# Keys and queries of three blocks loaded in 1 KB runs, with a re-made instruction plan

## The chip, the cores and the metric

The kernel runs on one core of a Trainium2 chip. The metric is the device time of one execution in microseconds (us), as the median of several executions. The profiled span is 1.8 to 1.9 us shorter than that time. The engines are PE (matmul), DVE (vector), ACT (scalar), POOL (GpSimd, which here writes the descriptors of the casting loads) and SP (which here issues stores and transposing DMAs). A single core gives no second die to compare with, so an execution counts as slow only if it is over 1.5% above the fastest; one execution of the kernel before was (317.86 us), and it is left out of every ratio.

## The reference

Sliding-window attention with a distance bias, then a feed-forward layer with a squared ReLU on its result:

```python
q, k, v: (8, 8, 576, 64) float32          # batch, heads, positions, head size
scores = q @ k.T / 8 - slope[h] * |i - j|  # kept where 0 <= i - j < 128
x = softmax(scores) @ v                    # -> (4608, 512)
out = relu(x @ w_in) ** 2 @ w_out          # w_in (512, 2048), w_out (2048, 512)
```

The kernel works in bf16 with fp32 accumulation. A "block" is 128 positions of one batch (or 64 at a batch's end); there are 40. Blocks 0 to 7 are the first of each batch.

## The kernel before

The program is a list of tasks, each with an engine, which a planner inside the kernel file sorts into one order before they are emitted. Block 0's keys and queries are staged in fp32 by SP and ACT; all other loads are casting DMAs from POOL:

```python
split = m < N_HW                      # N_HW = 1: block 0 alone
if split:
    ... nc.sync / nc.scalar .dma_start(view(stages[...], i)[:, r], source(src, m, split)[:, :, r])
    ... copy(kq[...], stages[...])    # cast and bring into head order, DVE
else:                                 # runs of 64 floats, 256 bytes
    nc.gpsimd.dma_start(view(kq[s_kq[m].idx], i), source(src, m, split))
```

Keys and queries must be transposed. Blocks below `N_PE = 8` do it on PE, the others by a DMA from SP:

```python
if m >= N_PE:
    nc.sync.dma_start_transpose(out=tile_of(sT)[:, :, 0:n], in_=kq[s_kq[m].idx][0:n, :])
    return
... for j in range(C): nc.tensor.transpose(...)        # 2 x 4 matmuls, then evictions
```

Stores go out from SP, the very last one from ACT. The pieces named in `HALVED` go out as two transfers of 64 rows:

```python
HALVED = [(7, 1), (7, 2), (7, 3)]
...
if (g, t) in HALVED:
    rows = [(r + 64 * i, 64 * i, 64) for r, _, _ in rows for i in range(2)]
for r, p, n in rows:
    (nc.scalar if final else nc.sync).dma_start(out[r:r + n, lo:hi], so.tile[p:p + n, 0:hi - lo])
```

Counting the transfers that SP and ACT issue: 4 staged loads, 32 transposes of keys and queries, 32 of attention rows and 44 stores, together **112**.

The softmax here doesn't subtract the row's maximum and nothing guards it: scores larger than these inputs give would overflow.

## Time and profile before

| | before |
|---|---|
| time, median of the first 3 executions | 313.23 us |
| profiled span | 311.14 us |
| PE busy | 302.0 us |
| start of the last matmul | 308.09 us |
| from there to the end of the span ("tail") | 3.05 us |

How PE's rate and the chain are read is shown with the prediction. Two more views are needed later. The first is the table of PE's waits between 6 and 20 us (engine, line, what it waited for; us in total, times, longest). PE waits in the head only for copies, never for a DMA:

```profile
PE xp L722 <- DVE x L702: 0.5, 2, 0.3
PE tp L513 <- DVE kq L304: 0.3, 1, 0.3
```

The second is the same table for SP's own queue in the last stretch of the span. L913 is the end of the program, where SP waits until every DMA has completed:

```profile
SPq L913 <- DMA out_dram<-osb: 1.4, 2, 1.1
```

The two waits that end with a store are the last two. I read the instructions of this closing sequence one by one from the trace (us after the start of the last matmul). SP makes nine waits in fixed order. The first is for loads alone and is over at 0.36 in every trace. Each of the other eight is for one pair of completion semaphores, of which one belongs to the hardware DMAs that SP and ACT issue; these are the eight waits meant below. The last store, from ACT, lands at 2.13, when seven of the eight are over. The eighth ends at 2.15. Then come POOL's clearing of the semaphores and the engines' final handshakes, and the span ends at 3.05.

### The profile page before, as it was taken

What the parts mean: (1) busy time and instruction counts of PE and PEld (TensorE: products, weight loads), DVE (VectorE), ACT (ScalarE), POOL (GpSimd) and SP (SyncE); (2) the same over time, 40 slices, a digit from 0 to 9 for tenths busy, and PEclk for the clock granted to TensorE, in tenths of its full rate; (3) what the DMA queues carried; (4) which work ended last, traced back from release to release, by engine and by line L of the source; (5) the groups of instructions that cost most, each with busy time, mean ns of one, the idle gap of its engine ahead of it and who ended that gap; (6) DMA issues with size and microseconds to landing.
All of it is one profiled execution on the core that took longest, in us unless ns stands there. A gap on an engine that the chain in (4) does not pass through costs nothing.

```text
span 311.1 us, 7054 instructions
## 1 busy us (share of the span) xinstructions
PE 302.0 (97%) x2748; PEld 174.1 (56%) x2792; DVE 166.0 (53%) x496; ACT 169.4 (54%) x324; POOL 106.2 (34%) x132
## 2 busy tenths in 40 slices
PE   8899999999999999999999999999999999999996
PEld 4579657676686744555455454555444444444443
DVE  6565367376667546877587665777222222222211
ACT  2676346496685556864588747664443444444400
POOL 8943586473821935604546463000000000000000
PEclk9999999999999999999999999999999999999999
DMA  9999999999999999999999999922111100011122
GB/s 133 161 206 207 174 195 174 166 194 158 160 164 189 160 127 203 161 101 184 121 167 170 175 169 185 193 68 57 46 34 56 45 36 34 36 36 34 34 88 83
DMA packets 166290, 39.54 MB, mean 127 GB/s; under 512 B 156400, under 2 KB 161776, under 8 KB 166256
## 3 DMA queue, kind: packets, MB, share of 16 engines
q0 software_dynamic: 115184, 18.10, 84.6%
q1 hardware_dynamic: 50640, 20.65, 36.0%
q8 instruction: 22, 0.36, 0.5%
q10 hardware_dynamic: 432, 0.33, 0.4%
q14 instruction: 12, 0.10, 0.1%
HBM read 36.70 MB, written 9.44 MB: 148 GB/s over the span
## 4 chain that ended last, share of the span: by engine, by line
PE 93%; DVE 2%; DMA 1%; issue 1%; ACT 1%; SPq 0%; DVEq 0%
PE o L850 40%; PE h L823 27%; PE h L806 14%; PE pv L676 6%; PE s L572 5%; DMA stage<-in_q_dram 1%; PE tp L513 1%; DVE x L702 1%; PE xp L722 1%; PE s L633 0%; ACT kqf L306 0%; ACT P L641 0%; DVE kqf L304 0%; DVE kq L304 0%; SPq L438 0%
## 5 line engine op out<-in xcount | busy, mean ns | idle before, releaser
L850 PE MATMUL o<-w_out_sb,g 128*128 128x512 bf16 (+2 forms) x564 | 137.7, 373 | 2.3 <-issue 1.1
L770 ACT ACTIVATE rt<-h 128x512 bf16<-128x512 f32 (+1 forms) x145 | 86.0, 600 | 88.2 <-PE h L823 66.9
L779 DVE TENSOR_TENSOR g<-rt 128x512 bf16<-128x512 bf16 (+1 forms) x145 | 60.3, 419 | 95.0 <-ACT rt L770 94.5
L823 PE MATMUL h<-xT,w_in_sb 128*128 128x512 bf16 x370 | 94.8, 379 | 0.8 <-issue 0.3
L850 PEld LDWEIGHTS <-g 128*128 128x128 bf16 x592 | 54.2, 98 | 56.9
L596 ACT ACTIVATE P<-s 128x512 bf16<-128x512 f32 x120 | 62.2, 605 | 12.9 <-PE s L572 12.9
L823 PEld LDWEIGHTS <-w_in_sb 128*128 128x128 bf16 x384 | 35.4, 98 | 39.9
L456 POOL DMA_DIRECT2D kq<-in_k_dram x39 | 33.4, 857 | 43.5 <-DMA kqT<-kq 29.0
L806 PE MATMUL h<-xT,w_in_sb 128*128 128x128 bf16 (+1 forms) x512 | 46.0, 246 | 0.0
L604 DVE TENSOR_TENSOR P<-P,masks 128x512 bf16<-128x512 bf16 x96 | 38.6, 418 | 11.6 <-ACT P L596 9.1
L806 PEld LDWEIGHTS <-w_in_sb 128*128 128x128 bf16 x512 | 39.0, 98 | 5.2
L461 POOL DMA_DIRECT2D vt<-in_v_dram x32 | 27.1, 847 | 31.6 <-PE pv L676 29.7
L456 POOL DMA_DIRECT2D kq<-in_q_dram x39 | 33.4, 856 | 6.4 <-PE h L806 2.0
L702 DVE TENSOR_TENSOR x<-pv,rec 128x256 bf16<-128x256 f32 (+1 forms) x80 | 32.0, 416 | 0.8
L676 PEld LDWEIGHTS <-P 128*128 128x128 bf16 (+1 forms) x576 | 24.2, 101 | 11.5 <-DVE g L779 1.3
L676 PE MATMUL pv<-vt,P 128*128 128x65 bf16 (+1 forms) x448 | 22.8, 194 | 0.0
L304 DVE COPY osb<-o 128x512 f32<-128x512 f32 (+1 forms) x19 | 13.0, 685 | 17.2 <-PE o L850 13.0
L306 ACT ACTIVATE osb<-o 128x512 f32<-128x512 f32 (+1 forms) x18 | 10.4, 580 | 21.5 <-PE o L850 21.5
L572 PEld LDWEIGHTS <-kqT 64*128 64x128 bf16 x448 | 12.4, 94 | 7.6 <-issue 6.8
L693 DVE RECIPROCAL rec<-pv 128x4 f32<-128x4 f32 (+1 forms) x80 | 12.3, 170 | 6.2 <-PE pv L676 5.6
L572 PE MATMUL s<-kqT 64*128 64x128 bf16 (+1 forms) x256 | 15.6, 210 | 0.0
L572 PE MATMUL s<-kqT,kqT 64*128 64x128 bf16 (+1 forms) x192 | 11.4, 210 | 0.1
(46 smaller groups left out, 102.7 us busy)
## 6 DMA issues: line engine op xcount, KB each, us to landing
out_dram<-osb SPq DMA_DIRECT2D x28, 256.0 KB, 5.2
kq<-in_k_dram POOLq DMA_DIRECT2D x31, 128.0 KB, 6.8
kq<-in_q_dram POOLq DMA_DIRECT2D x31, 128.0 KB, 7.0
vt<-in_v_dram POOLq DMA_DIRECT2D x24, 128.0 KB, 7.4
w_out_sb<-in_moe_w_out_dram POOLq DMA_DIRECT2D x4, 512.0 KB, 16.3
out_dram<-osb SPq DMA_DIRECT2D x14, 128.0 KB, 2.3
w_in_sb<-in_moe_w_in_dram POOLq DMA_DIRECT2D x3, 512.0 KB, 11.7
vf<-in_v_dram POOLq DMA_DIRECT2D x8, 128.0 KB, 6.7
```

The source lines that it names most:

```text
L456: nc.gpsimd.dma_start(view(kq[s_kq[m].idx], i), source(src, m, split))
L461: nc.gpsimd.dma_start(tile_of(s_v[m])[0:n, :, 0:D], source(v, m))
L572: nc.tensor.matmul(sS[2 * g2 + r].tile[:, jj * 256 + c0:jj * 256 + c0 + w], tile_of(s_kqT[mk])[rows, c, :], tile_of(s_kqT[mq])[rows, C + c ...
L596: nc.scalar.activation(flat(Pt[sP.idx]), sS[i].tile.rearrange("p (j t) -> p j t", j=2)[:, :, lo:hi], AF.Exp, bias=0.0, scale=scale)
L604: nc.vector.tensor_tensor(flat(Pt[sP.idx]), flat(Pt[sP.idx]), flat(masks), op=ALU.mult)
L676: nc.tensor.matmul(sv.tile[0:n, hi * (D + 1):(hi + 1) * (D + 1)], prob, tile_of(s_v[mk])[:, h, 0:D + 1], start=mk == parts[0][1], stop=mk ...
L702: nc.vector.tensor_tensor(o, heads(sv)[0:n, :, 0:D], sr.tile[0:n, :].unsqueeze(2).to_broadcast([n, 4, D]), op=ALU.mult)
L770: nc.scalar.activation(srt.tile[:, 0:n], slot.tile[:, 0:n], AF.Relu, bias=0.0, scale=1.0)
L779: nc.vector.tensor_tensor(o, i, i, op=ALU.mult)
L806: nc.tensor.matmul(slot.tile[:, f * w:(f + 1) * w], w_in_sb[:, cc, fc * 128:(fc + 1) * 128], xT[:, cc, lo:lo + w], start=cc == 0, stop=cc ...
L823: nc.tensor.matmul(slot.tile, w_in_sb[:, cc, fc * 128:(fc + 1) * 128], xT[:, cc, g * 512:(g + 1) * 512], start=cc == 0, stop=cc == C - 1)
L850: nc.tensor.matmul(slot.tile[:, 0:hi - lo], gt[:, fc, t * 128:(t + 1) * 128], w_out_sb[:, fc, lo:hi], start=fc == 0, stop=fc == FCB - 1)
```

## The change

Keys and queries of blocks 1 to 3 are read in runs of 1 KB into columns of the attention-row buffer `xT` that are not yet in use, and spread into head order by a copy on DVE or ACT. Block 0's staging moves to such columns too. Block 7 is now transposed by DMA (`N_PE = 7`). The planner's margins and priorities are new (with three small settings that are not shown, `N_CUT`, `N_PVH` and `NEAR`), and so the whole order. The core of the diff:

```diff
-FIRST = ["k0", "k1", "i0", "v0", "v1", "k2", "v2", "k3", "v3", "i1", ...]
+FIRST = ["k0", "k1", "v0", "k2", "k3", "i0", "v1", "i1", "v2", "i2", "v3", ...]
-N_PE = 8
+N_PE = 7
+N_ROW = 4
-SLACK = {"kq": 0.0, "kqT": 4500.0, "v": 2000.0, "x": 2500.0}
+SLACK = {"kq": 0.0, "kqT": 4000.0, "v": 5500.0, "x": 4000.0}
-LEAD = 1200
+LEAD = 600
...
-        split = m < N_HW
+        split = m < N_ROW
...
+        elif split:
+            def fetch_rows():
+                for i, src in enumerate((k, q)):
+                    nc.gpsimd.dma_start(rows_of(m, i).rearrange("s (r e) -> s r e", r=2), source(src, m, split))
+            ...
+            def spread(i):
+                copy(t_kq[m][i], kq[...].rearrange("s (i r d) -> s r i d", i=4, d=D),
+                     rows_of(m, i).rearrange("s (r i d) -> s r i d", r=2, d=D))
```

`HALVED` is unchanged, so the count of hardware DMAs goes from 112 to **113**.

## The prediction

> **What bounds the kernel now.** I read the page first, then the chain of waits in order of time, then the matmul and DVE timelines of the first 24 us, and last the table by stretches. The page's first part and the shares of the chain say who is the bound:
>
> ```profile
> PE 302.0 (97%) x2748; PEld 174.1 (56%) x2792; DVE 166.0 (53%) x496; ACT 169.4 (54%) x324; POOL 106.2 (34%) x132
> ...
> PE 93%; DVE 2%; DMA 1%; issue 1%; ACT 1%; SPq 0%; DVEq 0%
> ```
>
> PE is busy 302.0 of 311.1 us and carries 93% of the chain. Busy PE is not PE at its peak, so I checked the rate: in the chain, four output matmuls of 512 columns take 0.86 us (0.216 each), and 176 hidden-layer matmuls of 128 columns take 9.83 us (0.056 each). From 22.18 us on the chain has this and almost nothing else:
>
> ```profile
> by line: PE o L850 42.8%; PE h L823 29.0%; PE h L806 14.0%; PE pv L676 6.2%; PE s L572 5.8%; issue 1.1%; PE tp L513 0.7%; PE xp L722 0.3%; ACT osb L306 0.1%
> ...
> 22.18 9.83 PE h L806 x176
> ```
>
> So 286 us of the 311 are matmuls end to end; "issue" there is 1.1%, some 3.1 us, in pieces of 0.05 to 0.16 us where one kind of matmul follows another. No load, no eviction and no DVE wait is in that part of the chain. What is left to win lies before it. The matmul timeline of the head shows what PE does there:
>
> ```profile
> 5.24 1.39 PE L285 MATMUL tp<-warm 128*128 128x128 bf16 x22
> 6.95 0.84 PE L513 MATMUL tp<-ident,kq 128*128 128x128 bf16 x12 [0.32 <-DVE kq L304]
> ...
> 13.52 0.61 PE L806 MATMUL h<-xT,w_in_sb 128*128 128x128 bf16 x8
> ...
> 17.36 0.40 PE L722 MATMUL xp<-ident,x 128*128 128x128 bf16 x4 [0.21 <-DVE x L702]
> 17.59 1.06 PE L806 MATMUL h<-xT,w_in_sb 128*128 128x128 bf16 x16
> ```
>
> L285 are dummy matmuls on zeros, put in where the plan expects a gap. Up to 17.6 us PE runs the scores of blocks 0 to 3, dummies, and only 8 hidden-layer matmuls; from there it is dense. The table by stretches gives the transfers of the head (the last two columns are the DMA share and GB/s):
>
> ```profile
> 6.00:14.00 8.00, 6.64 (x96) 4.65 (x94) 5.17 (x21) 3.64 (x10) 8.00 (x11) 1.00 2.20 158
> 14.00:22.00 8.00, 7.45 (x104) 5.61 (x104) 6.02 (x29) 7.38 (x26) 4.72 (x6) 1.00 1.39 200
> ```
>
> In the first stretch keys, queries and values in 256-byte runs are moved, in the second the weights, in runs of 1 and 2 KB: 158 against 200 GB/s. The queue is never empty in either.
>
> **What the Trainium skill says.** "DMA: Bandwidth & Descriptors", section "Why small descriptors are slow (HBM only)", puts a fixed cost on each packet and counts 27% overhead for a 256-byte one. The trace agrees in size: 158 to 200 GB/s is 27% more. "SBUF — State Buffer", section "Who interferes with whom", says that a DVE copy in a 2-port mode and GpSimd block each other, which includes descriptors written for DMA. The new DVE copies between two SBUF tiles may be of this kind. The trace before holds two casts of the sort; the one at 6.10 took 0.79 us, the one at 3.69 took 0.57, while GpSimd was issuing. That fits, though it does not prove it. "Trainium Kernel Development and Optimization", opening section on reading a trace, calls matmul busy time a bad metric for distance from the roofline; that is why I use rates and not the 97%.
>
> **The change, part by part.**
>
> *Transfers.* Three blocks' keys and queries go from 256-byte to 1 KB runs. One such load is 131 KB as it lands. At 154 GB/s (the reading from 9 to 13 us) it takes 0.85 us, at 203 (the weights) 0.65. Six loads save 6 x 0.2 = 1.2 us of transfer time in the first 15 us. GpSimd's issue of them should drop from 0.89 us each towards the 0.77 of a weight piece. This engine is not the limit.
>
> *Copies.* The loaded rows must be spread into head order: six new copies of 128x512. The order of instructions shows four on DVE and two on ACT. From the 128x512 copies in the trace I take 0.4 us on DVE and 0.58 on ACT: 1.6 us of DVE and 1.2 of ACT. Their transposes come out permuted, so the PSUM evictions of blocks 1 to 3 become strided like those of block 0: 0.42 us on DVE where the plain ones take 0.28; six on DVE, +0.8 us. All 3.6 us fall between 6 and 15 us, where DVE is at 65% and in series with the scores. They lengthen the dependent chain of the early blocks.
>
> *Order.* The new order puts the score matmuls of block 0 behind both transposes of block 1, hence behind its loads and spreads. The first projection of block 0 comes after three spreads on DVE. I walked the order with durations of the trace: both halves of block 1 transposed by 8.4, scores of block 0 at 8.4 to 8.8 (before: 7.9 to 8.6), its exponentials 9.0 to 10.1 (before 8.7 to 9.7), its normalised output at 11.9 (before 11.1), scores of block 2 at about 13.4 (before 14.1), scores of block 3 at about 16.2 (as before), transposed outputs of blocks 1 and 2 by 17.0 (before 17.7). The head's attention is thus a little late at first and 0.7 us early at the end.
>
> *Weights.* In the new order 16 instead of 8 hidden-layer matmuls stand ahead of that point, then 32, 32 and 16 before the first 8 output matmuls end: 96 where the old order had 48. But the first of the 32 waits for the third piece of w_in (the order of waits shows that piece's semaphore there). By its place in the queue it needs 2,752 KB moved, counting what lands. Before, 586 KB had moved by 5 us (sum of the GB/s per us). The remaining 2,166 KB are 393 KB of values at 154 GB/s, 2.6 us, and 1,773 KB of long runs at 203, 8.7 us: moved at 16.3. From last byte to a waiting engine took 1.75 us for the second piece of w_in before (moved at 15.95 by that sum, released GpSimd at 17.7). Estimate of its landing: 18.0 us. That is later than the 17.0 of the chain, so dense work starts at 18.0, and the first eight output matmuls end 6.7 us later (80 hidden 4.5, 8 output 1.7, the rest 0.5): at 24.7. Before, that point came at 22.0 with 48 hidden matmuls fewer, which are 48 x 0.056 = 2.7 us. 22.0 + 2.7 = 24.7. **The head wins nothing** if this sum is right, and 1 us if the piece lands with the chain.
>
> *Block 7.* It is now transposed by DMA: eight matmuls of 0.056 us leave PE, 0.45 us that were in the dense part. This is certain to count, unless the transpose is late. One more DMA transpose (median 6.5 us to landing) joins a queue from which PE waits for nothing now.
>
> *Margins.* Larger slack for values and rows, loads asked for by a later key. In the dense part there is no wait for them to remove; the switches between kinds of matmul are 322 in the old order and 331 in the new. I give it 0 to 0.3 us. Sum: 0 + 0.45 + some 0.4 for the share of cases in which the piece lands earlier, so 0.9 us off 313.2.
>
> **The rivals.** (1) *The head gets 1 to 2 us shorter*, because the third piece lands by 17: for it speaks the 200 GB/s of long runs from the very start, against it the lag of 1.75 us which the trace shows. 311 us. (2) *Late copies*: the spreads, strided evictions and the chance of DVE and GpSimd blocking each other push the scores of block 1 back by a us or more; PE is in order, so everything behind waits. For it: three spreads stand before the first projections of block 0 on DVE. Against: the plan moved block 2 earlier to fill the time. 314 us. (3) *The transfer time saved is hidden anyway*: weights are needed at 18, 24 and 32 us, and they arrive just before; then only block 7 counts. 312.8 us. (4) *A new stall in the middle* from the new order, with one block's transpose moved to DMA. Against it: the queue runs through 200 us, but PE before never waited for it by more than 0.4 us.
>
> **The range.** I mix (3) as the main case with some of (1): 312.3 us. Rivals (1) and (2) span 310.7 to 314.0; the three runs of before spread 0.8 us themselves. Two per cent are 6.3 us. To win that, the head would have to lose 6 of its 11 us without useful matmuls, of which some 6 pass before the first query has landed (6.0 us). To lose it, a stall would have to appear in a plan with wider margins. Faster 0.02, same 0.965, slower 0.015.
>
> **What would show it right or wrong.** Right: six loads landing in under 5 us where those before took 4.8 to 6.6; the first 16 of the run of hidden matmuls starting near 18 us after a wait for w_in; 8 output matmuls finished near 24.7; dense PE thereafter with 1% of issue; one eighth fewer transposes. Wrong: that run starting by 17 (then 311 or less), or at 19 and beyond with waits for DVE or ACT copies ahead of it (then 314), or a PE wait over 0.5 us between 40 and 220 us. The sum on landing is the weakest step: it takes an arrival from bytes and a lag, and the staged query of block 0 (landed 6.0) may shift as well when long runs share its queues.

## The result, and the profile after

The changed kernel takes **314.5 us** (median of 4, 314.12 to 314.95), the kernel before on the same occasion 313.37 us (313.17 to 313.95). The ratio is 1.0034, 95% interval 1.0014 to 1.0053. (Ratios are the mean time of one kernel's fast executions over that of the other's in the same rounds, so not quite the ratio of these medians.) By the 2% rule this is "the same", but the time lies above the predicted range.

The two traces split the difference of the spans, 312.48 - 311.14 = 1.34 us:

| | before | after | difference |
|---|---|---|---|
| start of the last matmul | 308.09 | 308.57 | +0.48 |
| tail | 3.05 | 3.91 | +0.86 |

**PE.** The page's first part and the chain's shares no longer have "issue" in them. That is no gain: the trace before lacks 44 matmul records and this one lacks none, so the busy sum rises, 302.0 to 305.2, by records that were missing. PE busy can't be compared here; the start of the last matmul can.

```profile
PE 305.2 (98%) x2786; PEld 173.8 (56%) x2786; DVE 167.1 (53%) x498; ACT 170.8 (55%) x327; POOL 105.3 (34%) x132
...
PE 92%; POOL 2%; ACT 2%; DMA 2%; DVE 1%; issue 0%; POOLq 0%
```

POOL and DMA have entered the chain. The chain in order of time shows where (start, us, what): POOL writes the descriptors of six long key and query loads, of block 0's values and of the first piece of w_in first, and only then those of the values of block 1, for which PE waits.

```profile
3.81 2.83 POOL xT L468 x4
6.63 0.76 POOL w_in_sb L408
7.39 5.95 DMA vf<-in_v_dram
13.34 0.04 issue
13.38 0.40 PE pv L703 x8
```

PE's timeline of the head (start, us, engine, line, operation, output and inputs, count, and the idle time before with what ended it):

```profile
13.38 0.40 PE L703 MATMUL pv<-vf,P 128*128 128x65 bf16 x8 [0.99 <-DMA vf<-in_v_dram]
...
15.53 0.28 PE L703 MATMUL pv<-vf,P 128*128 128x65 bf16 x4 [0.31 <-DMA vf<-in_v_dram]
...
18.07 1.95 PE L833 MATMUL h<-xT,w_in_sb 128*128 128x128 bf16 x32 [0.28 <-DVE xT L311]
...
24.14 1.03 PE L877 MATMUL o<-w_out_sb,g 128*128 128x512 bf16 x4
```

Two waits for values, 1.3 us in sum, are new. The dense run starts at 18.07 and the eighth output matmul ends at 25.17 (24.14 + 1.03). In the kernel before that was 22.19, with 48 hidden matmuls fewer, 2.7 us:

```profile
21.16 1.03 PE L850 MATMUL o<-w_out_sb,g 128*128 128x512 bf16 x4
```

So the head is some 0.3 us worse. That is a difference of single traces, and traces of one kernel differ here by as much: the same point is at 22.19, 22.44 and 22.66 us in three traces with the old order (before, before_113, before_lane), at 25.17 and 25.61 in two of the changed kernel. What comes after it repeats: from there to the start of the last matmul the three old traces have 285.90 us and the two new ones 283.39, all within 0.02. With the 2.7 us of work moved ahead of the point, the new order is thus 0.2 us slower in the rest, although block 7's matmuls are gone from it.

**The transfers** themselves (issue to landing, from the table of DMAs issued in the first 16 us), before and then after:

```profile
kq<-in_k_dram POOLq DMA_DIRECT2D x3, 128.0 KB, 5.4
...
stage<-in_q_dram ACTq DMA_DIRECT2D x1, 128.0 KB, 3.4
stage<-in_q_dram SPq DMA_DIRECT2D x1, 128.0 KB, 4.5
```

```profile
xT<-in_k_dram POOLq DMA_DIRECT2D x3, 128.0 KB, 4.8
...
xT<-in_q_dram ACTq DMA_DIRECT2D x1, 128.0 KB, 4.7
xT<-in_q_dram SPq DMA_DIRECT2D x1, 128.0 KB, 4.8
```

The six loads are faster (4.75 to 5.15 us against 4.83 to 5.45), but the staged query of block 0, which the first scores wait for, is later: its two halves land at 6.15 and 6.32 where they landed at 4.82 and 6.00. The landing times that matter (us):

| | before | after |
|---|---|---|
| keys and queries of block 3 | 14.57 | 10.67 |
| first piece of w_in | 8.60 | 12.00 |
| values of block 1 | 10.33 | 13.34 |
| values of block 2 | 12.84 | 15.49 |
| third piece of w_in | 22.32 | 18.29 |

The mean interval from the landing of one such load to the next is 0.84 us before and 0.68 after.

**The spreads**, by form: four on DVE and two on ACT.

```profile
L311 DVE COPY kq<-xT 128x512 bf16<-128x512 bf16 x4 | 1.3, 325 | 0.0
L313 ACT ACTIVATE kq<-xT 128x512 bf16<-128x512 bf16 x2 | 1.3, 646 | 1.0 <-DMA xT<-in_q_dram 1.0
```

Together 2.6 us where the prediction had 2.8.

**The tail.** SP's waits at the end, and the DMA queues of the last stretch (queue, kind: packets, MB, share of 16 engines):

```profile
SPq L940 <- DMA out_dram<-osb: 1.8, 1, 1.8
...
q14 instruction: 1, 0.01, 0.3%
```

One wait, not two, ends with a store: the *first* of the eight. Read one by one (us after the start of the last matmul):

```
                              before                  after
last store lands (ACT)        2.13                    2.14
SP's waits after that         2.15                    2.16 2.22 2.28 2.34 2.40 2.46 2.52 2.59
POOL lets the engines go on   2.40                    2.83
POOL's DRAIN                  2.48 to 2.58            3.19 to 3.44
end of the span               3.05                    3.91
```

SP looks at the eight pairs of semaphores in a fixed order, and the trace shows the transfers take them in turn. 112 is a multiple of eight, so the last store had the last pair. The 113th transfer, block 7's transpose, moves it to the first pair, and seven more waits of 0.062 us follow its landing: 0.43 us. The other 0.43 us lie between POOL's handshake at 2.83 and the end of its DRAIN at 3.44: a pause of 0.35 us where the tail before has 0.06, and a DRAIN of 0.24 us instead of 0.10. The trace also has one 8 KB transfer on the queue that it calls "instruction", number 14, which the tail before does not have. It starts at 3.92, when the pause has long ended.

### The profile page after: what moved, and what is told of

It is laid out like the page before. It is cut to its first block, busy times and chain, and to the rows that moved or that the text cites. A ratio compares the mean times of both kernels' runs of the same rounds, so it can differ in the third digit from the quotient of the medians.

```text
span 312.5 us, 7105 instructions
## 1 busy us (share of the span) xinstructions
PE 305.2 (98%) x2786; PEld 173.8 (56%) x2786; DVE 167.1 (53%) x498; ACT 170.8 (55%) x327; POOL 105.3 (34%) x132
## 4 chain that ended last, share of the span: by engine, by line
PE 92%; POOL 2%; ACT 2%; DMA 2%; DVE 1%; issue 0%; POOLq 0%
PE o L877 40%; PE h L850 27%; PE h L833 13%; PE pv L703 6%; PE s L599 5%; DMA vf<-in_v_dram 2%; POOL xT L468 1%; ACT masks L351 1%; ACT rt L797 1%; PE tp L540 0%; PE xp L749 0%; ACT P L668 0%; DVE g L806 0%; POOL vf L488 0%; POOL w_in_sb L408 0%
## 5 line engine op out<-in xcount | busy, mean ns | idle before, releaser
L877 PE MATMUL o<-w_out_sb,g 128*128 128x512 bf16 (+2 forms) x592 | 142.2, 374 | 0.1
L850 PE MATMUL h<-xT,w_in_sb 128*128 128x512 bf16 x384 | 97.2, 379 | 0.0
L483 POOL DMA_DIRECT2D kq<-in_k_dram x36 | 30.4, 845 | 53.5 <-DMA kqT<-kq 39.5
L833 PE MATMUL h<-xT,w_in_sb 128*128 128x128 bf16 (+1 forms) x512 | 46.7, 246 | 0.4 <-DVE xT L311 0.3
L483 POOL DMA_DIRECT2D kq<-in_q_dram x36 | 30.5, 848 | 6.3 <-DVE g L806 2.0
L313 ACT ACTIVATE osb<-o 128x512 f32<-128x512 f32 (+1 forms) x21 | 12.2, 582 | 24.3 <-PE o L877 23.6
L311 DVE COPY osb<-o 128x512 f32<-128x512 f32 (+1 forms) x16 | 10.9, 684 | 14.4 <-PE o L877 11.1
```

What stands on the lines that cost most here:

```text
L833: nc.tensor.matmul(slot.tile[:, f * w:(f + 1) * w], w_in_sb[:, cc, fc * 128:(fc + 1) * 128], xT[:, cc, lo:lo + w], start=cc == 0, stop=cc ...
L850: nc.tensor.matmul(slot.tile, w_in_sb[:, cc, fc * 128:(fc + 1) * 128], xT[:, cc, g * 512:(g + 1) * 512], start=cc == 0, stop=cc == C - 1)
L877: nc.tensor.matmul(slot.tile[:, 0:hi - lo], gt[:, fc, t * 128:(t + 1) * 128], w_out_sb[:, fc, lo:hi], start=fc == 0, stop=fc == FCB - 1)
```

## The experiments

My theory of the 1.3 us: the tail's 0.86 comes from the count of transfers and from where POOL's program ends, and PE's part from the head, where the values of block 1 arrive late. The rivals: the tail's length has another cause or is chance; and the wait for values hides a next gate directly behind it, so that taking it away wins nothing. (Letters in the quoted expectations are those of each run.) For the experiments on order the executed order of a kernel was recorded and replayed with the moves told below; the replay without moves emits the same instructions. Table of all runs; "count" is that of hardware DMAs, "queue 14" says whether an instruction transfer on it starts at the end of the span (from 0.03 us before it to 0.25 us after it), "last" is the start of the last matmul in the profiled execution.

| run | count | queue 14 | last | tail | median (lowest) | ratio to before |
|---|---|---|---|---|---|---|
| before | 112 | no | 308.09 | 3.05 | 313.37 (313.17) | |
| after | 113 | yes | 308.57 | 3.91 | 314.5 (314.12) | 1.0034 |
| v1_early_b | 113 | yes | 308.37 | 3.93 | 314.2 (314.02) | 1.0006 |
| v12_early_b | 113 | yes | 308.78 | 3.91 | 314.5 (314.45) | 1.0011 |
| order_only_b | 113 | no | 309.46 | 3.49 | 314.82 (314.5) | 1.0024 |
| rows_only_b | 112 | yes | 309.91 | 3.40 | 315.11 (314.6) | 1.0029 |
| after_lane | 112 | yes | 310.30 | 3.48 | 313.88 (313.66) | 1.0020 |
| after_lane_pool | 112 | no | 311.16 | 3.07 | 315.14 (313.17) | 1.0037 |
| before_lane | 114 | no | 308.56 | 3.43 | 314.26 (313.62) | 1.0040 |
| block7_pe | 112 | yes | 309.21 | 3.41 | 314.4 (314.02) | 1.0027 |
| head_before | 112 | no | 315.95 | 3.06 | 320.85 (320.37) | 1.0207 |
| head_after | 112 | no | 311.82 | 3.05 | 316.22 (316.14) | 1.0057 |
| best | 112 | no | 312.36 | 3.07 | 314.66 (314.56) | 1.0027 |
| after_again | 113 | yes | 309.01 | 3.91 | 314.25 (314.05) | 0.9993 |
| before_113 | 113 | no | 308.35 | 3.47 | 313.72 (313.53) | 1.0015 |
| before_dma7 | 112 | no | 317.67 | 3.04 | 323.93 (322.49) | 1.0336 |
| v1_tail | 112 | no | 310.00 | 3.06 | 315.23 (313.25) | 1.0048 |

A caution on the ratios: 13 of the 45 fast executions of the kernel before on these occasions lie between 314.3 and 316.2 us instead of near 313.3. That widens the intervals to some 0.4% either way and brings about half of them across 1. For differences under 1 us I use the tail (which repeats to 0.03 us), the lowest time, and the stretch from the eighth output matmul to the last. The column "last" holds the head as well, and moves by 0.4 to 0.5 us from trace to trace of one order (308.09 to 308.56; 308.57 and 309.01).

### The order of the head

**order_only_b**: the changed order, but 256-byte runs and no spreads.

```diff
-N_ROW = 4
+N_ROW = 1        # and the tasks ck1..cq3 dropped from the replayed order
```

> The changed kernel's order of all instructions, with the keys and queries of blocks 1 to 3 loaded in 256-byte runs as before and no spreads. If the new order is at fault and the long runs help: each of the six loads takes 0.84 us instead of 0.70 on the queue, the values of block 1 land 0.8 us later, at 14.2, and the kernel takes 315.2. If the spreads and strided evictions are at fault: PE gains what they cost, 314 or less.

Measured: last matmul at 309.46, 0.5 to 0.9 us later than in the two traces with long runs; values of block 1 at 13.78 (expected 14.2); median 314.82 us (expected 315.2), with a tail that is 0.42 shorter than the changed kernel's. PE's waits between 6 and 20 us:

```profile
PE pv L924 <- DMA vf<-in_v_dram: 2.4, 2, 1.6
```

So in the new order the long runs are worth 0.5 to 0.9 us, and the wait for values comes from the order: it stands there, larger, with 256-byte runs too. Here the staged query landed at 5.59, so its delay to 6.32 goes with the long runs.

**rows_only_b**: the other half alone, the old order with 1 KB runs, a spread put in front of each block's first use.

```diff
-N_ROW = 1
+N_ROW = 4        # in the replayed order of the kernel before, with ck1..cq3 inserted
```

> The order of the kernel before, with the 1 KB runs, the six spreads and the strided evictions put into it, block 7 transposed on PE. If the long runs are a gain that the new order gives away: values of block 3 and the weights land 0.6 to 1 us earlier than in the kernel before, 312.5 to 313.2. If the copies cost what the transfers save: 313.4 to 314.

A miss: 1.4 to 1.8 us worse at the last matmul than the three traces of the old order, instead of a gain, and all of it in the head (the rest takes 285.90 us, as theirs). The staged query landed at 6.64, the scores of block 0 started at 8.61 instead of 7.86, and the spreads stood on the in-order DVE ahead of block 0's normalisation. PE's waits of the head:

```profile
PE xp L970 <- DVE x L950: 0.7, 2, 0.5
PE s L881 <- DVE kqf L532: 0.4, 2, 0.2
PE tp L513 <- DVE x L950: 0.4, 1, 0.4
```

Neither half gains alone; each makes the other bearable.

**v1_early_b** and **v12_early_b**: the changed kernel with the values of block 1 issued right after those of block 0; in the second, those of block 2 also ahead of the second piece of w_in.

```diff
-lv0 ... lkq2 lkq3 w_in0 lv1 w_in1 lv2
+lv0 lv1 ... lkq2 lkq3 w_in0 w_in1 lv2          # v1_early_b
+lv0 lv1 ... lkq2 lkq3 w_in0 lv2 w_in1          # v12_early_b, a hidden unit of block 0 later as well
```

> The changed kernel with one transfer moved: the values of block 1 are issued right after those of block 0, ahead of the keys and queries of blocks 2 and 3. Theory A (the 0.99 us that PE stood before the value product of block 1 is the loss): that wait goes, all that follows comes 0.9 us earlier, 313.6 us, so level with the kernel before. Theory B (the next gate stands at the same time: the values of block 2, which landed at 15.49, and the product of block 2 started at 15.53): the wait of block 1 goes, the wait before block 2 grows by as much, and the time stays at 314.4, within 0.2 us of the changed kernel.

> As v1_early_b, and the values of block 2 issued before the second piece of w_in, with the one hidden-layer unit that needs that piece moved behind the first unit of block 1. Theory A expects the same as for v1_early_b or worse. Theory B: neither product waits for values; scores of block 3 about 1 us earlier (15.7 where they were 16.74), the long run of hidden-layer matmuls from 17.1 where it was 18.07, and 313.6 us unless the third piece of w_in, landed at 18.3, becomes the gate, then 313.9.

The waits for values are gone in both, and little is won: 0.2 us at the last matmul in the first, 0.2 us lost in the second, both less than the two traces of the changed kernel differ by. The times, 314.2 and 314.5 us, are theory B's for the first run and a miss for the second. A load put forward puts another back. In the first, keys of block 2 land at 9.59 instead of 8.63, and their spread then stands ahead of block 0's outputs on DVE. In the second PE waits for ACT instead:

```profile
PE pv L925 <- ACT P L890: 0.5, 2, 0.3
PE h L1055 <- DVE xT L533: 0.3, 1, 0.3
PE h L1055 <- ACT rt L1019: 0.2, 1, 0.2
```

The 1.3 us of waits was thus not 1.3 us of time: the next gate stood directly behind. It was not the gate that theory B named: PE no longer waits for the values of block 2 either.

### The tail

**after_lane** takes one hardware DMA away, **after_lane_pool** also lengthens POOL's program by three tiny instructions.

```diff
-HALVED = [(7, 1), (7, 2), (7, 3)]
+HALVED = [(7, 2), (7, 3)]
         for t in done:
             t.emit()
+        for _ in range(3):                 # after_lane_pool only
+            nc.gpsimd.memset(pad, 0.0)
```

> The changed kernel with the store of output piece 1 of the last tile whole instead of halved: one hardware-DMA transfer fewer, 112 in place of 113, so that the last store is again the last of its eight completion semaphores to be waited for. Theory A (closing waits count): after the last store has landed one wait is left instead of eight, the tail from the start of the last matmul to the end of the span falls from 3.91 to about 3.48 us, the time from 314.5 to about 314.1 us. Rival (the longer tail comes from something else in the changed program): tail stays at 3.9, 314.5 us.

> As after_lane, with three tiny memsets more at the end of the POOL program, so that its closing instructions stand elsewhere in the instruction stream. If POOL's pause of 0.36 us in the closing sequence comes from where its program ends, it goes, the tail falls to about 3.05 us as before the change, and the time to about 313.6 us. Rival (the pause has another cause): tail 3.48 us, 314.1 us, as after_lane.

The tails came out as expected, 3.48 and 3.07 us. The lowest times follow: 314.05 to 314.12 for the changed kernel (on two other occasions), 313.66, 313.17, steps of about 0.4 and 0.5 us. But several executions (one of five and three of five) took 315 to 316 us, the profiled ones among them. The wait table of the second, between 100 and 250 us, shows what they spent:

```profile
PE s L600 <- DMA kqT<-kq: 2.2, 2, 1.7
```

Scores wait for a transposing DMA. Its median from issue to landing was 8.6 us in this execution, 7.4 in the changed kernel's own trace, 6.5 in the kernel before. None of the 10 executions of the changed kernel as it stands did this. Over all runs in the changed order, 9 of the 22 executions with 112 transfers and block 7 by DMA (after_lane, after_lane_pool, best, v1_tail) took over 315 us, and none of the 27 of after, after_again, v1_early_b, v12_early_b and block7_pe. (order_only_b, 2 of 6 from a higher level, is left aside.) That looks like more than chance, though not all of these ran on one occasion and no run shows what links the two. So the repair is shown for the tail, not for the median time.

**before_lane** and **before_113** raise the count in the kernel before, to 114 and 113. The first halves a piece that holds two half-blocks, so it writes wrong rows: its result is wrong, its timing stands.

```diff
-HALVED = [(7, 1), (7, 2), (7, 3)]
+HALVED = [(7, 0), (7, 1), (7, 2), (7, 3)]      # before_lane: 114
+HALVED = [(6, 3), (7, 1), (7, 2), (7, 3)]      # before_113
```

> The kernel before with one store more (a fourth halved store: 113 hardware-DMA transfers in place of 112) and nothing else. Theory A: the last store's semaphore is now the first waited for, seven or eight waits follow its landing, the tail rises from 3.05 to about 3.48 us, the time by 0.4 us to about 313.8. Rival: tail 3.05 us, no change of time.

> The kernel before with one more store, of another tile in two halves: 113 hardware-DMA transfers instead of 112, correct result. Theory (the last store's semaphore becomes the first of eight to be waited for): seven waits of 0.062 us more after its landing, tail 3.05 + 0.43 = 3.48 us, time 313.3 + 0.4 = 313.7 us. Rival: tail 3.05 us, no change.

In the first I had counted 113; with 114 the last store has the second pair, six waits more follow, and 3.05 + 6 x 0.062 = 3.42; measured 3.43. In the second seven waits follow, the tail is 3.47, expected 3.48. SP's waits in the second show the first-pair pattern:

```profile
SPq L913 <- DMA out_dram<-osb: 1.8, 1, 1.8
```

The old kernel, correct and otherwise untouched, gets 0.42 us of tail from one transfer more. Tail and count go together as the order of the waits says. That settles the first half of the longer tail.

**The second half** rests on the table. In every run with an instruction transfer on queue 14 at its end the tail is 0.33 to 0.46 us longer than in one of the same count without. POOL executes 201 instructions in the changed kernel, in after_lane, v1_early_b and v12_early_b, and pauses before its DRAIN; 202 in rows_only_b and block7_pe, and pauses one instruction earlier; 203 to 206 in the others, and no pause shows after the last store. So the pause keeps its place in POOL's stream, after the 196th instruction, and the program moves past it. That POOL waits for instructions there is a guess. It can't be for the transfer in the table: that starts 0.7 to 1.0 us after the pause is over, at the end of the span or after it. What the runs show is that transfer, pause and count go together, and that three instructions more remove both; what POOL waits for is open.

### Block 7

**block7_pe**: the changed kernel, in its order, with block 7's transposes back on PE.

```diff
-N_PE = 7
+N_PE = 8         # kqT7 replaced by tp7.0, tp7.1 and two evictions in the replayed order
```

> The changed kernel, in its own order, with the transposes of block 7 back on PE (8 matmuls of 64 ns by the rows of the other blocks, 2 evictions) in place of one transposing DMA. Theory: PE's part rises by 0.45 us to a last matmul at about 309.0, the tail falls by 0.43 because 112 transfers end on the last-waited semaphore, together 314.5 us, no change. Rival (the move to DMA was worth its 0.45 us at the end): 315.0 us. Rival (the DMA transpose held up PE elsewhere): last matmul not later than 308.6 us and the time about 314.1.

From the eighth output matmul to the last it takes 283.93 us against 283.39: block 7 on PE costs 0.54 us, a little over the 0.45. (The last matmul itself, at 309.21, is 0.2 to 0.6 us later than in the two traces of the changed kernel.) The tail fell by 0.50, 0.43 by the count and 0.07 with POOL's program one instruction longer (3.41 against after_lane's 3.48), and the time did not change (lowest 314.02 against 314.05). What block 7 saved on PE its transfer took back at the end.

**before_dma7**: block 7 by DMA in the kernel before, planned anew.

```diff
-N_PE = 8
+N_PE = 7
-HALVED = [(7, 1), (7, 2), (7, 3)]
+HALVED = [(7, 2), (7, 3)]
```

> The kernel before with block 7 transposed by DMA and one halved store fewer (112 transfers), its plan made anew by the same planner; the order up to the transposes of block 7 is the old one. Prediction's step (block 7 is certain to count 0.45 us): last matmul at 307.6 us, tail 3.05, time 312.8 us. Rival (the order that follows costs it again in switches or a wait for the transpose): last matmul at 308.1 us or later, 313.3 us or more.

It cost 10 us, so neither expectation holds. The priorities are tuned to one order and do not survive a new plan; the question whether the old order could have had the 0.45 us is not answered. How it lost so much is worth seeing, below.

### Splices

**head_before** takes the order of the kernel before up to the transposes of block 4 and that of the changed kernel from there; **head_after** the reverse. Both have the tail repaired.

```diff
-order = recorded_after
+order = recorded_before[:tp4.0] + [t for t in recorded_after if t not in head]      # head_before
+order = recorded_after[:tp4.0] + [t for t in recorded_before if t not in head]      # head_after
```

> A splice: the head of the kernel before (loads in 256-byte runs, its order of instructions up to the first transposes of block 4 at 37 us), from there on the order of the changed kernel, block 7 by DMA, with one store fewer (112 hardware-DMA transfers) and three tiny memsets on POOL so that the tail is as before. Theory (the changed order after the head costs PE about 0.6 us, the block 7 move saves 0.45): last matmul at about 308.25 us, tail 3.05, time about 313.3 us. Rival (the later order costs nothing, the changed head is all of it): last matmul at about 307.6 us, time about 312.7 us.

> The other splice: the head of the changed kernel (1 KB runs and spreads) up to the first transposes of block 4, from there on the order of the kernel before, block 7 on PE, 112 hardware-DMA transfers, the three memsets on POOL. Theory (the new head costs 0.3 us net, the later order another 0.6 that is now gone): last matmul at about 308.4 us, tail 3.05, time about 313.5 us. Rival (the 0.6 us after the head follow from the head itself, late evictions and shifted loads): last matmul at 309.0 us or later, time 314.1 us or more.

Both missed, and both are inconclusive: loads and buffers at the seam fit neither half, and stalls there (from 37 to 60 us) drown the half microsecond that was asked for. What the first shows is another thing. Its stretches around the seam (busy us of PE, PE's loads, DVE, ACT and POOL with counts, then the granted clock, DMA share, GB/s):

```profile
42.00:44.00 2.00, 1.15 (x22) 0.73 (x21) 1.43 (x4) 1.61 (x4) 2.00 (x3) 1.00 2.53 166
44.00:45.00 1.00, 0.52 (x6) 0.28 (x6) 0.94 (x4) 0.46 (x1) 1.00 (x2) 0.77 1.62 218
45.00:51.00 6.00, 5.09 (x33) 3.25 (x34) 2.32 (x10) 1.20 (x2) 4.48 (x6) 0.50 2.00 145
51.00:52.00 1.00, 1.00 (x10) 0.81 (x8) 0.07 (x1) 0.37 (x1) 0.00 (x0) 0.81 4.32 114
```

After a stretch in which PE was busy little over half of the time the granted clock falls to 0.50 for 6.8 us, in which matmuls take about twice their time, on top of the gaps. before_dma7 does the same at 86 to 93 us, again for 6.8 us, after four microseconds at 52% busy; there matmuls of 65 columns start 0.055 us apart where they started 0.03 apart before. Being busy little over half is not enough by itself: after_lane_pool has 56% from 135 to 139 us and keeps 1.00.

### Versions meant to be faster

**best** (tail repaired, values of blocks 1 and 2 early, block 1's transpose and first hidden unit ahead of the scores of block 3), **after_again** (the changed kernel unaltered, as its neighbour) and later **v1_tail** (tail repaired, values of block 1 early).

```diff
-... pv2.0 u0.0.1 pv2.1 b3 s3 xp1.0 xp2.0 u0.1.0 u0.0.2
+... pv2.0 xp1.0 u0.1.0 pv2.1 b3 s3 xp2.0 u0.0.1 u0.0.2      # best, PE; copies moved likewise
-lv0 ... lkq2 lkq3 w_in0 lv1
+lv0 lv1 ... lkq2 lkq3 w_in0                                 # v1_tail; both: HALVED and the memsets of after_lane_pool
```

> The changed kernel with the tail mended (112 transfers, three memsets on POOL), values of blocks 1 and 2 loaded ahead of the second piece of w_in, and the transpose and first hidden unit of block 1 put ahead of the scores of block 3 on PE, with their copies ahead on DVE and ACT. Theory: tail 3.05 us (0.86 less than the changed kernel), head 0.3 us shorter, last matmul at about 308.2, time about 313.3 us, equal to the kernel before. Rival (another gate takes the place again): last matmul at 308.6 to 308.8, time 313.6 to 313.8 us.

> The changed kernel unaltered, to have its time on the same chip as the three others and a second trace. Expected: last matmul at 308.6 us, tail 3.91, time 314.5 us.

> The changed kernel with 112 transfers, three memsets more on POOL and the values of block 1 loaded right after those of block 0. Theory (the closing sequence was all that separated it from the kernel before): tail 3.05, last matmul at 308.4 to 308.6, time 313.2 to 313.5 us in its undisturbed executions. Rival (the tail repair is given back elsewhere): 314 us.

best missed: its tail is 3.07, but its lowest time is 314.56, so the moves in the head lost what the tail won. after_again repeated the changed kernel, tail 3.91 to the hundredth. v1_tail reached 313.25 once in six executions, the level of the kernel before; the others took 314.1 to 317.0. No version beats the kernel before. The changed kernel with its tail repaired comes near it in its best executions: 313.17 (after_lane_pool) and 313.25 (v1_tail) against lowest times of 313.1 and 312.78 on the same occasions.

## Why the prediction was wrong, point by point

The time came 2.2 us over the 312.3 and 0.5 over the range. Of the 2.2 us, 0.86 are the tail, and the rest is PE, for which 0.9 us of gain were forecast and 0.48 of loss came. By its own steps:

- **"This is certain to count, unless the transpose is late"** (block 7, 0.45 us) is the step that failed. The eight matmuls did leave PE (0.54 us by block7_pe) and the transpose was not late (landed at 53.3, first used at 62.2). But the step looked for its price only in PE's waits on the queue. The transfer that it adds is the 113th, and costs 0.43 us in the closing waits (shown by before_113, 0.42, and after_lane, 0.43). block7_pe shows both sides: PE later, tail shorter, time unchanged.
- **The end of the program was left out of the sum.** The text treats the span as PE's end plus a constant. The constant rose by 0.86, the second half of it from POOL's program being three instructions shorter. With the tail as before, 314.5 would have been 313.6, inside the range. It is the largest single term of the miss.
- **"The head wins nothing"** was nearly right in size: eighth output matmul at 25.17 for a predicted 24.7. That is luck, for the path to it was wrong. The third piece of w_in landed at 18.29, as estimated (18.0), but the first of the 32 hidden matmuls doesn't need it; it was the transposed output of block 1 that was awaited, at 18.07. I had misread whose semaphore stood there. (The lag of 1.75 us in that sum also ran to GpSimd's next instruction; the second piece itself had landed at 17.21, 1.26 us after the 15.95.) I walked the order with the old durations but never worked out when the values of block 1 land; their place in the queue, behind six key and query loads, made 1.0 us of wait. v1_early_b showed that even this was hardly the bound.
- **"Some 0.4 for the share of cases in which the piece lands earlier"** did not come: the piece landed at 18.29 and 18.80 in the two traces of the changed kernel, and it was not the gate.
- **Transfers**: six loads save 6 x 0.16 us, not 6 x 0.2. The 0.2 came from comparing with the weights' rate.
- **"The staged query ... may shift"**, named as the weakest step, did: from 6.00 to 6.32 us (6.64 in rows_only_b, 5.59 with short runs in the new order). The first scores wait for it.
- **Copies**: the spreads' 2.6 us were sized well (2.8). On DVE they took 0.26 to 0.50 us each; whether GpSimd held up the longer ones, no run isolates. rows_only_b, whose order makes no room for them, doesn't separate their cost: of its loss of 1.4 to 1.8 us, 0.75 is there when the scores of block 0 start, from the late staged query, and the rest comes with PE's waits for DVE.
- **Margins, "0 to 0.3 us"**: no gain but a loss. From the eighth output matmul on, the new order takes 0.2 us more for the same work, and block 7 had saved 0.54 there; so the rest of the new order costs about 0.7 us. No run isolates what in it does; the splices were meant to and failed. The head's 0.3, this 0.7 and block 7's -0.54 make the 0.48 of the last matmul.

Rival 3 (the transfer time saved is hidden) held for the head, and v1_early_b shows something of rival 2 behind the values: spreads ahead of other work on DVE. Rival 4 did not come: the trace lists no PE wait between 30 and 308 us. None had the tail. That the change moves the time by under 2% was right.

## What to carry to other kernels

Look at what happens after the last matmul before adding or taking a transfer: here the place of the last store in the closing waits was worth 0.43 us, nearly as much as eight matmuls (0.54 us). A wait in the head is worth only the distance to the next gate behind it, so find that gate before counting the wait. A tuned order is one piece: half of a change put into another order, or a splice of two, can cost more than the whole change was about.

## What the Trainium skill lacked or had wrong

- No page has the price of the waits on DMA completions at the end of a program: eight waits in fixed order, 0.062 us each, so that the number of hardware DMAs modulo eight moved the end by 0.42 us (tails of 3.05, 3.47 and 3.43 us for 112, 113 and 114 transfers in the kernel before).
- "DMA: Bandwidth & Descriptors", section "Queues, rings and completion order", calls queue row 14 internal to the runtime. Seven traces have an 8 KB transfer of kind "instruction" on queue 14 at the end of the span, and in these seven, and no others, POOL pauses for 0.35 to 0.37 us shortly before. No page has the size of such a pause or says at which point of an engine's program it falls; what causes it is open here too.
- The same page, section "Why small descriptors are slow (HBM only)", counts 27% overhead for 256-byte packets. Between these loads in runs of 256 bytes and of 1 KB the runs show 0.84 against 0.68 us each, 24%, so it comes near. The page has no figure for what longer runs cost a transfer of another queue at the same time (staged query 6.00 to 6.32 us).
- "TensorE: Matmul & The Clock Gate", Part 1, lets the clock fall to half after an idle window of about 3.4 us. The half clock agrees (0.50), but PE was not idle: before_dma7 was 52% busy over the four microseconds before, with no gap over 1.0 us. A later passage of Part 1 does know such falls from many short gaps, but gives no share of busy time; here 52% fell and 56% with a single gap of 1.7 us did not (after_lane_pool).
